# More buffers for scaled weight words and raw heads, and PSUM as the first stop of twenty weight pieces

## Chip, cores and metric

The kernel runs on one core of a Trainium2 chip. The metric is the device time of one execution in microseconds. Before the change it is 1238.18 us (median of 3 runs, 1236.21 to 1244.08).

## The reference

Decayed causal attention over 64 heads (8 batches of 8 heads, 576 tokens of 64 numbers each) is followed by a normalised feed-forward layer on the 4608 tokens of width 512.

```python
# q, k, v: (8, 8, 576, 64); f: (8, 8, 576)
scores = matmul(q, k.T) / 8
cum = cumsum(log(clip(f, 1e-4, 1)))
scores = where(causal, -1e9, scores + cum[:, None] - cum[None, :])
attn = exp(scores - max(scores)); attn = attn / (sum(attn) + 1e-9)
x = matmul(attn, v)                      # heads side by side: (8, 576, 512)
xn = (x - mean(x)) / sqrt(var(x) + 1e-6) * g_ln
out = x + maximum(xn @ w_ch1, 0) @ w_ch2 # w_ch1: 512 x 2048, w_ch2: 2048 x 512
```

The two weight matrices arrive as float64 words. [...]

## The kernel before

**Three streams in one order.** The order of all instructions is written out by hand. Time is cut into slots, four for each head (u counts them, t = 1 to 4 is the slot in the head). In a slot a string of letters (`ORDERS`) says in which order the pieces of work are issued: `W` and the fill letters `w`, `g`, `f` for the weights' preparation, `Q` scores, `S` mask and row minimum, `e` exponential, `B` row sums and scaling, `t`, `h`, `l` transposes of the probabilities and their copies, `A`, `F`, `a` probabilities times v, `P` loads and splits for the next heads, and `M`, `r`, `m`, `N`, `R` the feed-forward part. Each engine runs its own instructions strictly in this order. So does SyncE, which issues every transfer: an issue that has to wait for a buffer holds up all transfers behind it.

**Weights.** The class `WPrep` prepares 32 pieces of 128 x 512, by turns one of the first matrix (layer 1) and one of the second (layer 2). A call of `tick` moves several pieces by one step each. In the order of a piece's life the steps are:

- `load`: SyncE brings 128 x 512 words of 8 bytes into a `wr` buffer (3 of them, lines 147 and 152).
- `scaled` (line 163): ScalarE scales the upper halves and writes them to a `wy` buffer (5 of them, `W_FLOAT`).
- `decode` (lines 173 and 174): VectorE shifts the lower halves in place, then shifts the scaled words and ors the lower halves into them, in place in `wy`. After this the `wr` buffer is free.
- `colsum` and `centre` (lines 186 and 194), for layer 1 alone: TensorE makes column sums, VectorE multiplies by the gains and adds the centring.
- `high` (line 211): ScalarE rounds to the short format that TensorE takes.
- `low` (line 215): GpSimd subtracts the rounded part, which leaves the rest. After this the `wy` buffer is free.
- `keep` (line 220): the rest of layer 2 goes to DRAM.

A layer 2 piece is scaled at the end of one tick, decoded in the next, and its `low` comes three ticks after the decoding; a layer 1 piece takes five. The line that scales piece n + 1 stands in the fill queue of tick n, behind the decoding of piece n.

**Attention.** The first eight heads are plain: their q and k go to the multiplier as they are. From head 8 on q and k are split into a high and a low part. For these heads line 315 allots the `raw` buffer (one), line 316 loads it in slot 4 two heads ahead, `prep_a` to `prep_c` (lines 334 to 346, slots 1 to 3 one head ahead) split it: ScalarE casts into `hi` (lines 334 and 341), GpSimd subtracts (lines 337 and 345). The last of these is also the last use of the `raw` buffer. Scores (lines 365, 367, 368) land in PSUM, VectorE adds the mask (391), ScalarE takes the exponential (402), VectorE adds to the row sum and inverts it (407, 408), GpSimd scales (409), TensorE transposes (415), ScalarE copies out of PSUM (465). Lines 478 and 500 multiply by v; line 531 (`xs`) copies the result out of PSUM.

**Feed-forward.** From slot 35 on (`FIRST_MOE`) chunks of 256 tokens run between the heads: `mm1` (577 to 579), the two parts of the rectified result (585, 590), `mm2` (599 to 601) into two accumulators. These are the two PSUM banks tagged `acc0` and `acc1`, first allotted in `mm2`; the other six banks are shared by everything else under the tag `b`.

Of the kernel before, what the change touches and what calls it, by code (L numbers as in the profile page):

```python
# [8 lines left out]
F32 = mybir.dt.float32  # L9
F32R = mybir.dt.float32r  # L10
U32 = mybir.dt.uint32
I32 = mybir.dt.int32
AF = mybir.ActivationFunctionType
ALU = mybir.AluOpType

B, H, S, D = 8, 8, 576, 64
DM, DFF = H * D, 4 * H * D
P = 128
# [15 lines left out]
WARM = 36  # L34

W_SLOTS, W_CHANGE, W_TICKS = 1.6, 34, 0.95
W_RAW, W_FLOAT = 3, 5
W_BORROW = 2
W_SUMS = 2
W_ASIDE = 5  # L40
FILL = {"f": 3, "g": 2, "w": 1}
RSTD = 6

# [13 lines left out]
def attn_moe(ctx: ExitStack, tc: tile.TileContext, qk, v, f, g, w1, w2, out):  # L59
    nc = tc.nc  # L60
# [4 lines left out]
    ps = ctx.enter_context(tc.tile_pool(name="ps", bufs=1, space=bass.MemoryType.PSUM))  # L65

    wpool = ctx.enter_context(tc.tile_pool(name="early", bufs=1))
    late = ctx.enter_context(tc.tile_pool(name="late", bufs=1))
# [6 lines left out]
    def m2(name, dt):  # L75
        return work.tile([P, 512], dt, tag="m2", bufs=11, name=name)
# [9 lines left out]
    for i in range(WARM):  # L86
# [4 lines left out]
        out=mask[:, S - P :], in_=mask[:, S - P :], pattern=[[-1, P]], base=0,  # L91
# [42 lines left out]
    class WPrep:  # L134
# [8 lines left out]
        def load(self, n):  # L143
            layer, j = self.items[n]
            raw = wpool.tile([P, 2 * DM], U32, tag="wr", bufs=W_RAW, name=f"wr{layer}_{j}")
            if layer == 1:
                nc.sync.dma_start(
                    out=raw.rearrange("p (k f) -> p k f", k=KT),
                    in_=w1.bitcast(U32)[:, 2 * j * P : 2 * (j + 1) * P].rearrange("(k p) f -> p k f", p=P),
                )  # L150
            else:
                nc.sync.dma_start(out=raw, in_=w2.bitcast(U32)[j * P : (j + 1) * P, :])
            halves = raw.rearrange("p (n t) -> p n t", t=2)
            self.d[n] = {"hw": halves[:, :, 1], "lw": halves[:, :, 0]}

        def scaled(self, n):
            layer, j = self.items[n]
            d = self.d[n]
            if layer == 1 and self.tick_no < W_BORROW:
                d["y"] = m2(f"wy{layer}_{j}", U32)  # L160
            else:
                d["y"] = wpool.tile([P, DM], U32, tag="wy", bufs=W_FLOAT, name=f"wy{layer}_{j}")
            nc.scalar.activation(d["y"].bitcast(F32), d["hw"].bitcast(F32), AF.Prelu, scale=2.0**-112, alpha=2.0**32)

        def decode(self, n):
            layer, j = self.items[n]
            d = self.d[n]
            y, low = d["y"], d["lw"]
            d["w"] = y.bitcast(F32)
            ve = nc.vector  # L170

            return [
                lambda: ve.tensor_scalar(out=low, in0=low, scalar1=29, scalar2=None, op0=ALU.logical_shift_right),
                lambda: ve.scalar_tensor_tensor(
                    out=y, in0=y, scalar=3, in1=low, op0=ALU.logical_shift_left, op1=ALU.bitwise_or
                ),
            ]

# [85 lines left out]
        late = None  # L264
# [32 lines left out]
    def new_xq(name, dt):  # L297
        xq = work.tile([66, S], dt, tag="xq", bufs=2, name=name)
        nc.gpsimd.memset(xq[64:66, :].bitcast(F32), 1.0)
        return xq  # L300

    def load(n):
        h = Head()
        h.n, h.plain, h.full = n, n < NPLAIN, n < NFULL
        if h.plain:
            h.kl = work.tile([66, S], F32, tag="kl", bufs=2, name=f"kl{n}")
            if len(xfs) < 2:
                xfs.append(new_xq(f"xf{n}", F32))
            h.xq = xfs[n % 2]
            nc.sync.dma_start(out=h.xq[0:64, :], in_=qk[n][0:64, 0, :])  # L310
            nc.sync.dma_start(out=h.kl[0:64, :], in_=qk[n][0:64, 1, :])
            if n > 0:
                nc.sync.dma_start(out=h.kl[64:66, :], in_=cumd[n])
            return h
        h.raw = late.tile([P, 2, S], F32, tag="raw", bufs=1, name=f"raw{n}")
        nc.sync.dma_start(out=h.raw, in_=qk[n])
        return h

# [316 lines left out]
    def run_later(k):  # L635
        while later and k > 0:
            later.pop(0)()
            k -= 1
# [23 lines left out]
    class Moe:  # L662
# [21 lines left out]
        low = []  # L684
# [63 lines left out]
    def start_head(n):  # L748
        hd[n] = load(n)
# [9 lines left out]
    for u, slot in enumerate(slots):  # L759
# [4 lines left out]
        if slot is not None:  # L764
            n, t = slot
            h = hd[n]
# [6 lines left out]
        def piece(c):  # L773
# [34 lines left out]
            elif c == "L":  # L808
                run_later(RSTD)
            elif c == "M" and want:  # L810
# [38 lines left out]
    while moe.left() > 0 or moe.prev is not None:  # L849
        if moe.can(2 * FT):  # L850
            moe.first()
            moe.first_high()
            moe.first_low()
        run_later(RSTD)
        moe.fetch_low(ALL)
# [40 lines left out]
```

## Time and profile before

| | |
|---|---|
| Median of 3 runs | 1238.18 us |
| Profiled execution | 1240.83 us |
| Its span, first to last instruction | 1239.0 us |
| TensorE busy | 1215.1 us |
| VectorE busy | 767.6 us |
| ScalarE busy | 647.6 us |
| GpSimd busy | 427.3 us |
| Mean granted TensorE clock | 0.988 |

All times in the lines of the profile are microseconds, and `mean ns` is nanoseconds. PE is TensorE's multiplication, PEld its weight loads, DVE is VectorE, ACT ScalarE, POOL GpSimd, SP SyncE; a q behind the name means the sequencer of that engine. `out<-in` names the tiles, and L163 is line 163. A row of a timeline has the start, the duration, the engine and line, and in brackets the idle time of that engine just before it with what ended it. A row of waits has total, number and longest. A row by windows has the window, its length, the busy time of PE, PEld, DVE, ACT and POOL with the number of their instructions, the granted clock, the share of the transfer engines' time, and GB/s. A granted clock of 0.50 means that multiplications ran at half speed.

### The profile page before, as it was taken

The numbers are of one execution on the slowest core, as the hardware profiler recorded it, in microseconds if no ns is written. First come the engines' busy times: TensorE is split into PE (matmuls) and PEld (weight loads), VectorE is DVE, ScalarE is ACT, GpSimd is POOL, SyncE is SP. The second block draws the span as 40 slices with busy tenths as digits, with TensorE's granted clock in tenths as the row PEclk, the third lists the DMA queues.
The fourth block names the chain that finished last, engine by engine and source line by source line (L and its number), as shares of the span: only waits on it lengthen the run. The fifth ranks groups of instructions, "written<-read, shape, count | busy, mean of one in ns | idle before, by whom it ended". The sixth has DMA issues, their size and how long they took to land.

```text
span 1239.0 us, 25554 instructions
## 1 busy us (share of the span) xinstructions
PE 1215.1 (98%) x8140; PEld 1080.7 (87%) x8140; DVE 767.6 (62%) x2884; ACT 647.6 (52%) x1920; POOL 427.3 (34%) x533
## 2 busy tenths in 40 slices
PE   8998999999999999999999999999999999999998
PEld 5555789888999999999999999999999999999997
DVE  5786737576766767676767676767676765233232
ACT  5777655455656555555565555555555653112111
POOL 3567553344333434343433343343444330000000
PEclk8997999999999999999999999999999999999999
DMA  6875744444544554544454554545454543443532
GB/s 181 235 234 179 240 141 133 148 126 140 163 154 154 172 166 148 152 158 142 152 161 155 166 158 145 157 138 160 150 152 145 169 149 103 135 129 111 154 111 94
DMA packets 138359, 190.79 MB, mean 154 GB/s; under 512 B 31216, under 2 KB 80624, under 8 KB 138224
## 3 DMA queue, kind: packets, MB, share of 16 engines
q1 hardware_dynamic: 138224, 189.15, 49.5%
q8 instruction: 65, 1.06, 0.4%
q14 instruction: 70, 0.57, 0.2%
HBM read 157.46 MB, written 23.36 MB: 146 GB/s over the span
## 4 chain that ended last, share of the span: by engine, by line
PE 89%; DVE 3%; ACT 2%; DMA 2%; POOL 1%; issue 1%; SPq 0%; DVEq 0%; POOLq 0%; ACTq 0%
PE h L577 11%; PE h L578 11%; PE h L579 11%; PE acc L599 11%; PE acc L600 10%; PE acc L601 10%; PE tr L415 7%; PE o L500 6%; PE s L367 3%; PE s L368 3%; PE o L478 2%; PE xp L415 1%; DMA raw<-in_qk_dram 1%; PE s L365 1%; PE pc L186 1%
## 5 line engine op out<-in xcount | busy, mean ns | idle before, releaser
L409 POOL TENSOR_SCALAR p<-p,st 64x64 f32<-64x64 f32 (+4 forms) x320 | 171.8, 540 | 555.1 <-DVE st L408 217.9
L577 PE MATMUL h<-x,w1h 128*128 128x256 f32 x1152 | 330.1, 287 | 3.5 <-DVE st L407 2.7
L578 PE MATMUL h<-x,w1h 128*128 128x256 f32 x1152 | 326.2, 283 | 0.9 <-DVE st L407 0.6
L579 PE MATMUL h<-x,w1l 128*128 128x256 f32 x1152 | 325.2, 282 | 0.0
L585 ACT ACTIVATE hh<-h 128x256 fp32r<-128x256 f32 x288 | 110.5, 384 | 281.7 <-PE h L579 280.4
L590 DVE SCALAR_TENSOR_TENSOR hh<-h,hh 128x256 fp32r<-128x256 f32 x288 | 121.5, 422 | 187.0 <-ACT hh L585 174.2
L599 PE MATMUL acc<-w2h,hh 128*128 128x512 f32 x576 | 228.1, 396 | 0.4 <-ACT hh L585 0.4
L600 PE MATMUL acc<-w2s,hh 128*128 128x512 f32 x576 | 226.6, 393 | 0.0
L601 PE MATMUL acc<-w2h,hh 128*128 128x512 f32 x576 | 226.0, 392 | 0.0
L577 PEld LDWEIGHTS h<-x,w1h 128*128 128x128 f32 x1152 | 218.4, 190 | 8.5 <-DVE st L407 3.0
L578 PEld LDWEIGHTS h<-x,w1h 128*128 128x128 f32 x1152 | 218.5, 190 | 4.7 <-DVE x L562 1.7
L579 PEld LDWEIGHTS h<-x,w1l 128*128 128x128 f32 x1152 | 218.3, 189 | 0.0
L402 ACT ACTIVATE p<-p,st 64x64 f32<-64x64 f32 (+4 forms) x320 | 178.3, 558 | 54.0 <-DVE st L391 51.3
L465 ACT CAST ph<-tr 64x128 fp32r<-64x128 f32 (+4 forms) x416 | 117.9, 332 | 131.1 <-PE tr L415 100.8
L415 PE MATMUL tr<-identr,p 128*128 128x128 f32 (+1 forms) x896 | 141.2, 274 | 5.5 <-ACT xs L531 2.3
L391 DVE CUSTOM_DVE_ANT_0 p<-s,mask 64x64 f32<-64x64 f32 (+4 forms) x320 | 130.2, 419 | 7.7 <-PE s L368 2.8
L470 DVE TENSOR_TENSOR ph<-tr,ph 64x192 fp32r<-64x192 f32 x208 | 62.6, 301 | 114.5 <-ACT ph L465 111.6
L601 PEld LDWEIGHTS acc<-w2h,hh 128*128 128x128 f32 x576 | 108.3, 188 | 25.5 <-DVE st L407 0.2
L415 PEld LDWEIGHTS tr<-identr,p 128*128 128x128 f32 (+1 forms) x896 | 101.2, 131 | 29.2 <-POOL p L409 10.3
L599 PEld LDWEIGHTS acc<-w2h,hh 128*128 128x128 f32 x576 | 109.0, 189 | 13.1 <-ACT hh L585 0.6
L600 PEld LDWEIGHTS acc<-w2s,hh 128*128 128x128 f32 x576 | 109.3, 190 | 12.4
L367 PE MATMUL s<-hi 128*64 128x64 f32 x336 | 110.6, 351 | 2.8 <-POOL hi L345 2.6
(80 smaller groups left out, 1805.6 us busy)
## 6 DMA issues: line engine op xcount, KB each, us to landing
w2s<-w2d SPq DMA_DIRECT2D x288, 256.0 KB
raw<-in_qk_dram SPq DMA_DIRECT2D x56, 576.0 KB
wr<-in_w_dram SPq DMA_DIRECT2D x32, 512.0 KB
vr<-in_v_dram SPq DMA_DIRECT2D x64, 160.0 KB
out_dram<-xt SPq DMA_DIRECT2D x36, 256.0 KB
xq<-hi SPq DMA_DIRECT2D x56, 144.0 KB
xa<-xs SPq DMA_DIRECT2D x32, 160.0 KB
w2d<-wl SPq DMA_DIRECT2D x16, 256.0 KB
```

Source lines behind the costliest of these rows:

```text
L367: mm(sp, h.hi[:, 0, q0 : q0 + m], h.hi[:, 1, a:z], start=True, stop=False)
L391: nc.vector.tensor_tensor_reduce(out=pt[:m, a:z], in0=sp, in1=mask[:m, off + a : off + z], scale=-SCALE, scalar=3.0e38 if i == 0 else st[: ...
L402: nc.scalar.activation(pt[:m, :w], pt[:m, :w], AF.Exp, bias=st[:m, i : i + 1], scale=-1.0, accum_out=st[:m, 2:3])
L409: nc.gpsimd.tensor_scalar(out=pt[:m, :w], in0=pt[:m, :w], scalar1=st[:m, 3:4], scalar2=1.0, op0=ALU.mult, op1=ALU.mult)
L415: nc.tensor.transpose(out_, in_, ident[:m, :m])
L577: mm(ph, w1h[:, k, fs], c.x[k][:, 0, :], start=(k == 0), stop=False)
L578: mm(ph, w1h[:, k, fs], c.x[k][:, 1, :], start=False, stop=False)
L579: mm(ph, w1l[:, k, fs], c.x[k][:, 0, :], start=False, stop=(k == KT - 1))
L590: nc.vector.scalar_tensor_tensor(out=h[:, 1, :], in0=ph, scalar=0.0, in1=h[:, 0, :].bitcast(F32), op0=ALU.max, op1=ALU.subtract)
L599: mm(c.acc[i], h[:, 0, ts_], w2h[:, j, :], start=(j == 0), stop=False)
L600: mm(c.acc[i], h[:, 0, ts_], low, start=False, stop=False)
L601: mm(c.acc[i], h[:, 1, ts_], w2h[:, j, :], start=False, stop=(j == FT - 1))
```

## The change

`scaled` writes the first twenty pieces (`W_PSUM`, ten of each layer) to PSUM, to the banks tagged `acc0` and `acc1` by turns. The second instruction of `decode` then reads its first operand there and writes its result to the `wy` buffer, as before. Later pieces are scaled in place as they were. There are nine `wy` buffers and two `raw` buffers. The memory for them comes from the scratch that is set aside for transfers whose descriptors are made on the core: it is set to 1024 bytes. The order of the instructions is the same.

```diff
-W_RAW, W_FLOAT = 3, 5
+W_RAW, W_FLOAT = 3, 9
...
+W_PSUM = 20
...
-            nc.scalar.activation(d["y"].bitcast(F32), d["hw"].bitcast(F32), AF.Prelu, scale=2.0**-112, alpha=2.0**32)
+            d["z"] = d["y"]
+            if n < W_PSUM:
+                d["z"] = ps.tile([P, DM], U32, tag=f"acc{n % 2}", bufs=1, name=f"wz{layer}_{j}")
+            nc.scalar.activation(d["z"].bitcast(F32), d["hw"].bitcast(F32), AF.Prelu, scale=2.0**-112, alpha=2.0**32)
...
-            y, low = d["y"], d["lw"]
+            y, z, low = d["y"], d["z"], d["lw"]
...
-                    out=y, in0=y, scalar=3, in1=low, op0=ALU.logical_shift_left, op1=ALU.bitwise_or
+                    out=y, in0=z, scalar=3, in1=low, op0=ALU.logical_shift_left, op1=ALU.bitwise_or
...
-        h.raw = late.tile([P, 2, S], F32, tag="raw", bufs=1, name=f"raw{n}")
+        h.raw = late.tile([P, 2, S], F32, tag="raw", bufs=2, name=f"raw{n}")
...
-    nc = bacc.Bacc("TRN2", target_bir_lowering=False, num_devices=1)
+    nc = bacc.Bacc("TRN2", target_bir_lowering=False, num_devices=1, dynamic_dma_scratch_size=1024)
```

## The prediction

> **What bounds the kernel now.** I read the page first, then the waits of TensorE and ScalarE in the stage with the idle time, then that stage's timeline engine by engine, last the granted clock in it.
>
> ```profile
> span 1239.0 us, 25554 instructions
> PE 1215.1 (98%) x8140; PEld 1080.7 (87%) x8140; DVE 767.6 (62%) x2884; ACT 647.6 (52%) x1920; POOL 427.3 (34%) x533
> ```
>
> TensorE is busy for 98% of the span, and its instruction order is fixed in the program. So the time is its work, plus its idle time, plus what a lower clock costs. The next rows split the span in three stretches (the busy columns are in the order PE, PEld, DVE, ACT, POOL; then the granted clock).
>
> ```profile
> 7.00:36.00 29.00, 25.07 (x122) 16.62 (x120) 20.02 (x76) 20.12 (x56) 11.27 (x19) 0.88 0.68 197
> 36.00:131.00 95.00, 85.47 (x417) 55.29 (x417) 70.69 (x245) 71.68 (x210) 59.20 (x65) 0.89 0.72 216
> 131.00:1239.00 1108.00, 1099.52 (x7582) 1003.72 (x7580) 674.39 (x2562) 553.27 (x1654) 353.67 (x439) 1.00 0.48 147
> ```
>
> What the change could free for TensorE lies in the middle row: the first holds the start, before the buffers are short, and in the last TensorE idles for under 1%. TensorE idles 95 - 85.5 = 9.5 us and loses 11% of the clock, some 10.4 us. About 20 us is therefore the most that can be won. Without those losses the stage would be 75 us long, with ScalarE busy for 71.7 of them: 95% of a queue that runs in order and waits on others. Winning all of it is unlikely for that reason alone.
>
> **Part 1, nine buffers.** Each weight piece takes a `wy` buffer at line 163 and gives it back when GpSimd has subtracted at line 215. With five, one comes free per tick and one is taken per tick, so the ScalarE instruction waits for the subtraction issued in the same tick. Queued behind it on ScalarE are the copies (`xs`, `ph`) that give PSUM banks back to TensorE. ScalarE's waits in the stage:
>
> ```profile
> ACT wy L163 <- POOL wl L215: 5.1, 5, 2.1
> ACT ph L465 <- PE tr L415: 3.9, 4, 1.5
> ACT wy L163 <- POOL w1l L215: 2.4, 3, 1.0
> ```
>
> Nine buffers cover four more ticks, so all eight waits (7.5 us of ScalarE) go. Only some of them reach TensorE. The first clear one:
>
> ```profile
> 46.35 0.68 ACT L163 ACTIVATE wy<-wr 128x512 f32<-128x512 f32 x1 [1.19 <-POOL wl L215]
> 46.93 0.41 ACT L531 COPY xs<-o 64x320 f32<-64x320 f32 x1
> ```
>
> ```profile
> 47.48 0.49 PE L415 MATMUL tr<-identr,p 128*64 128x128 f32 x3 [1.18 <-ACT xs L531]
> ```
>
> Without the wait, `wy` starts at 45.16 (46.35 - 1.19), `xs` 0.58 later at 45.74 and ends at 46.15, before TensorE gets there at 46.30 (47.48 - 1.18). That gap goes, and with it the half clock that follows:
>
> ```profile
> 48.49:51.91 3.42, 3.42 (x11) 1.68 (x9) 2.36 (x11) 2.29 (x8) 0.53 (x1) 0.50 0.21 80
> 92.87:96.28 3.41, 3.36 (x8) 1.62 (x9) 1.62 (x7) 3.18 (x10) 2.31 (x3) 0.50 0.17 39
> 113.35:123.59 10.24, 9.52 (x35) 7.28 (x36) 6.17 (x19) 7.69 (x23) 8.32 (x8) 0.50 0.67 224
> ```
>
> Half a clock for 3.42 us of matmuls is 1.7 us. 1.18 + 1.71 less 0.1 for the next `ph` copy: **2.8 us**. The second place:
>
> ```profile
> 90.64 0.67 ACT L163 ACTIVATE wy<-wr 128x512 f32<-128x512 f32 x1 [1.20 <-POOL wl L215]
> ```
>
> ```profile
> 91.76 0.49 PE L415 MATMUL tr<-identr,p 128*64 128x128 f32 x3 [1.16 <-ACT xs L531]
> 92.92 0.68 PE L478 MATMUL o<-ph,vr 64*64 64x256 f32 x1 [0.67 <-ACT ph L465]
> ```
>
> The 1.16 goes. The 0.67 behind it stays, because ScalarE still has copies and casts to do first.
>
> ```profile
> 99.20 0.24 PE L367 MATMUL s<-hi 128*64 128x64 f32 x1
> ```
>
> The half clock from 92.87 may go too, yet I count nothing for it: the matmul of 99.20 reads `hi` of raw head 8, which GpSimd makes last in a chain (exponential, row sum, scaling, subtraction) that does not run on TensorE. What TensorE gains on the way it then waits. So **1.16 us**. The third place:
>
> ```profile
> 100.87 0.68 ACT L163 ACTIVATE wy<-wr 128x512 f32<-128x512 f32 x1 [0.33 <-POOL wl L215]
> ```
>
> ```profile
> 103.87 1.16 PE L186 MATMUL pc<-wy,gneg 128*128 128x128 f32 x8 [0.54 <-ACT xs L531]
> 104.87 0.49 PE L415 MATMUL tr<-identr,p 128*64 128x128 f32 x3
> 106.54 0.68 PE L478 MATMUL o<-ph,vr 64*64 64x256 f32 x1 [1.19 <-ACT ph L465]
> ```
>
> The 0.33 stands on ScalarE ahead of the `xs` copy that TensorE awaits for 0.54: **0.3 us**. The longest of the eight, 2.1 us, falls beside the GpSimd chain of part 2, and I count nothing for it.
>
> **Part 2, two raw heads.** The load of raw head n+2 keeps its place in the program, one slot after the last use of head n+1. A second buffer therefore helps only where SyncE stood waiting for that use. This happened once:
>
> ```profile
> SPq L316 <- POOL hi L345: 1.4, 1, 1.4
> ```
>
> ```profile
> 99.18 0.33 SPq L316 DMA_DIRECT2D raw<-in_qk_dram x1
> ```
>
> ```profile
> 103.40 0.42 ACT L531 COPY xs<-o 64x320 f32<-64x320 f32 x1
> 105.11 0.67 ACT L334 CAST hi<-raw 128x576 fp32r<-128x576 f32 x1 [1.29 <-DMA raw<-in_qk_dram]
> ```
>
> It was the load at 99.18, of head 9. It could issue 1.4 earlier, so ScalarE does not stand still for 1.29. Behind that cast queue `wy` and then `ph`, whose input TensorE finished at 105.36 (104.87 + 0.49). With 1.29 less in front of it `ph` is no longer held up by ScalarE but by that end, and of the 1.19 us gap before 106.54 some 0.3 is left, the length of the copy: **0.9 us**. It does not grow from there:
>
> ```profile
> 108.16 0.53 POOL L409 TENSOR_SCALAR p<-p,st 128x320 f32<-128x320 f32 x1 [3.15 <-ACT hi L341]
> 108.66 1.40 POOL L337 TENSOR_TENSOR kl<-raw,hi 64x576 fp32r<-64x576 f32 x1
> 110.02 1.72 POOL L215 TENSOR_TENSOR wl<-wy,w2h 128x512 fp32r<-128x512 f32 x1
> 111.73 0.80 POOL L409 TENSOR_SCALAR p<-p,st 128x448 f32<-128x448 f32 x1
> 112.61 1.40 POOL L345 TENSOR_TENSOR hi<-raw,hi 64x576 fp32r<-64x576 f32 x1
> ```
>
> ```profile
> 114.07 0.31 PE L367 MATMUL s<-hi 128*64 128x64 f32 x1 [2.56 <-POOL hi L345]
> ```
>
> GpSimd runs without a break from 108.16 to 114.0, and TensorE waits for its end. Its start moves by the same 0.9. Whatever else TensorE wins before (the half clock at 106.5 too) turns into a longer wait here, from 2.56 towards 4 us. The smaller scratch costs nothing: all data goes by the hardware queue, and no transfer is issued by GpSimd.
>
> **Part 3, twenty pieces in PSUM.** No row of before has ScalarE write scaled words to PSUM, or this shift-and-or read them there. The nearest rows:
>
> ```profile
> L174 DVE SCALAR_TENSOR_TENSOR wy<-wy,wr x32: 676/912/2074, 8.4 to 155.0; 128x512 uint32<-128x512 uint32 x32
> 0.00:98.60 98.60, 20.66 (x20) 0.93 0.70 208
> L658 DVE SCALAR_TENSOR_TENSOR xt<-acc,rs,xt x36: 740/744/751, 204.7 to 1235.3; 128x512 f32<-128x512 f32 x36
> L163 ACT ACTIVATE wy<-wr x32: 643/666/710, 7.4 to 152.5; 128x512 f32<-128x512 f32 x32
> L173 DVE TENSOR_SCALAR wr<-wr x32: 407/412/1476, 7.8 to 154.0; 128x512 uint32<-128x512 uint32 x32
> ```
>
> Line 174 reads two SBUF tensors and spreads from 676 to 2074 ns; line 658 has the same shape and reads one of the two from PSUM, and keeps to 740 to 751. The first twenty (the second row, of line 174 alone) took 20.66 us. At 0.744 they take 14.9: **5.8 us of VectorE**; the bounds are 20 x 0.676 (7.1 saved) and no change. ScalarE's own instruction I leave at 0.666; 20 times its spread is from 0.5 us gained to 0.9 lost. VectorE has 24 us free in the stage, so most of this lies beside other work. It can only count where TensorE waits on a chain through VectorE:
>
> ```profile
> 80.60 0.27 PE L415 MATMUL tr<-identr,p 128*64 128x128 f32 x1 [0.67 <-DVE st L391]
> ```
>
> I give it **0.2 us** of this gap; 0 and 0.67 are its ends.
>
> The Trainium skill (SBUF — State Buffer, section Who interferes with whom) says that a VectorE instruction with two SBUF inputs contends with a GpSimd instruction that reads SBUF, and that a `tensor_scalar` in its two-port mode does so too. By the first sentence the spread of line 174 ends for all twenty, as the rows suggest. By the second, which speaks against the change, line 173 in front of it (407 to 1476 ns in its row) stays exposed. The page has no price for that; the sum above does not use it.
>
> Two waits are added. Line 163 of piece n waits until line 174 of piece n-2 has read the bank, and the first `mm2` of the feed-forward part waits for pieces 18 and 19. Behind the first stand `xs`, `ph` and the exponentials, behind the second all of TensorE. Both are long over:
>
> ```profile
> L174 DVE SCALAR_TENSOR_TENSOR wy<-wy,wr x3: 679/815/1464, 83.2 to 91.5; 128x512 uint32<-128x512 uint32 x3
> L599 PE MATMUL acc<-w2h,hh x1: 396/396/396, 132.1 to 132.1; 128*128 128x512 f32 x1
> ```
>
> Pieces 17 to 19 are read at 83.2 to 91.5. Piece 17 is through at 84.7, 4.8 us before line 163 of piece 19 could run (89.4), and the first accumulation starts 40 us later.
>
> **Sum:** 2.8 + 1.16 + 0.3 + 0.9 + 0.2 = 5.4 us. The profiled execution took 1240.8 us and its span was 1239.0, so it becomes 1235.4. It was 2.6 us above the median of the runs, 1238.2; from the median the forecast is **1232.8 us**.
>
> **Rivals.** *All of it is won.* If ScalarE and GpSimd keep up, the stage loses its 9.5 us of idle time and the 10.3 us of half clock: 1238.2 - 19.8 = 1218.4. For it: eight ScalarE waits and 5.8 us of VectorE go at once. Against it: the unbroken GpSimd chain above and the 95%. A part way, 9 to 14 us, is likelier than the end.
>
> *Another wait takes over.* TensorE arrives earlier and waits for the exponentials or for `hi`; the half clocks return at new gaps. Gain 0 to 3 us, 1235 to 1238. For it: in the stage ScalarE is already busy for 75% and the chain passes from engine to engine.
>
> *Slower, by the clock.* The gap in front of 114.07 grows from 2.6 towards 4 us. The half clock after it, three windows of 3.41 us, could last longer while TensorE's matmuls there are on the path. Each window more costs 1.7 us, so from four more (6.8 us against 5.4) the kernel is slower: 1238.2 + 1.4 = 1239.6, two more still 1243. For it: the 10.24 us row, against single windows elsewhere. Against it: TensorE is nearly always busy after 114, and then single windows were enough. The Trainium skill (TensorE: Matmul & The Clock Gate, section What's actually happening) has full clock return after one busy window of about 3.4 us; by that rule this case has no room. The trace agrees at 48.49 and 92.87 and disagrees at 113.35, where three windows passed with 9.5 of 10.2 us busy.
>
> *The second raw buffer does nothing* (the load waits for bandwidth): 0.9 less, 1233.7, inside the forecast's own range.
>
> **How the numbers follow.** One per cent, 12.4 us, is about what a measurement of this kernel can tell from no change. Forecast (3 to 9 us gained) 0.50; most of it won (9 to 20) 0.25, of which over 12.4 us 0.17; another wait (0 to 3) 0.17; slower 0.08, of which over 1% 0.04. So faster 0.17, same 0.79, slower 0.04. The range runs from 1225, 13 us gained, to 1241, where the clock case begins to cost; the unknown prices of part 3 move it by under 2 us.
>
> **What would show it.** Right: no wait of line 163 on line 215 in the waits; line 174's first twenty near 0.745 us with no spread; no gap and full clock at the first place; raw head 9 issued within 0.5 us of the weight load ahead of it; and a wait for `hi` of about 4 us still there before the matmul of 114.07, now about 5 us earlier. Wrong: that wait gone or the middle stage shorter by over 9 us (GpSimd did not bind), a new ScalarE wait on the weight loads, or the 131 to 1239 stage changed by over 2 us, for which I have no cause.

## The result and the profile after

The median is 1233.24 us (1229.54 to 1236.59, 11 runs) against 1240.27 us for the kernel before over 11 runs beside it (1236.21 to 1244.08). The ratio is 0.9944 (95% interval 0.9935 to 0.9954), which is 6.9 us faster (5.7 to 8.1), where 5.4 us were forecast. (The 1232.8 us of the forecast were counted from the median of three runs of before, which lies 2.1 us below that of the eleven.) The profiled execution of after has a span of 1233.4 us, 5.6 us less than that of before.

The page of after, and its three stretches (window, length, busy time of PE, PEld, DVE, ACT, POOL, granted clock, transfer share, GB/s):

```profile
span 1233.4 us, 25519 instructions
PE 1209.6 (98%) x8140; PEld 1079.6 (88%) x8140; DVE 763.8 (62%) x2884; ACT 647.0 (52%) x1920; POOL 425.6 (35%) x533
```

```profile
7.00:36.00 29.00, 24.36 (x113) 16.64 (x111) 18.00 (x71) 17.87 (x50) 10.37 (x17) 0.82 0.62 176
36.00:131.00 95.00, 86.69 (x468) 58.45 (x467) 71.81 (x271) 76.23 (x226) 61.46 (x70) 0.96 0.80 240
131.00:1233.40 1102.40, 1093.51 (x7542) 999.48 (x7540) 671.39 (x2542) 550.43 (x1645) 350.62 (x436) 1.00 0.47 147
```

In the middle stretch TensorE now does 468 multiplications in 95 us where it did 417, but these are not the same ones. Between the same two matmuls, the last of them the first of the feed-forward part, before and after read:

```profile
25.95:130.57 104.62, 95.09 (x466) 61.14 (x464) 78.13 (x273) 79.64 (x233) 64.08 (x71) 0.90 0.70 211
28.03:124.29 96.26, 87.95 (x467) 58.16 (x465) 72.15 (x272) 78.56 (x232) 62.58 (x71) 0.96 0.77 229
```

Of the 8.4 us between them most is clock: two windows of 3.41 us at half clock instead of six, which is worth 6.8 us. The idle time is hardly less, 8.3 against 9.5 us.

**The buffer wait is gone.** ScalarE's waits from 28 to 131 us (total, number, longest) have no line any more in which the scaling (now L167) waits for GpSimd's subtraction (now L219):

```profile
ACT p L406 <- DVE st L395: 8.0, 12, 1.5
ACT w1h L215 <- DVE wy L198: 3.7, 5, 1.0
ACT ph L469 <- PE tr L419: 3.7, 6, 0.8
ACT hi L338 <- DMA raw<-in_qk_dram: 2.3, 2, 1.9
ACT xs L535 <- PE o L482: 1.5, 2, 0.8
ACT wy L167 <- DMA wr<-in_w_dram: 1.1, 1, 1.1
```

At the first place the scaling follows the exponential at once, `xs` follows it, and TensorE's transposes start without a gap (ScalarE, then TensorE):

```profile
46.35 0.19 ACT L406 ACTIVATION_READ_ACCUMULATOR p<-p,st 128x1 f32 x1
46.44 0.63 ACT L167 ACTIVATE wz<-wr 128x512 f32<-128x512 f32 x1
47.01 0.41 ACT L535 COPY xs<-o 64x320 f32<-64x320 f32 x1
```

```profile
48.04 0.57 PE L419 MATMUL tr<-identr,p 128*64 128x128 f32 x3
```

**The operations that PSUM changed.** By line, with minimum, median and maximum in ns; `wz` are the twenty pieces that go through PSUM, `wy<-wy,wr` the twelve that don't:

```profile
L178 DVE SCALAR_TENSOR_TENSOR wy<-wz,wr x20: 674/684/692, 8.4 to 89.0; 128x512 uint32<-128x512 uint32 x20
L178 DVE SCALAR_TENSOR_TENSOR wy<-wy,wr x12: 676/1284/2070, 95.3 to 149.1; 128x512 uint32<-128x512 uint32 x12
```

```profile
L167 ACT ACTIVATE wz<-wr x20: 602/626/649, 7.0 to 87.3; 128x512 f32<-128x512 f32 x20
L167 ACT ACTIVATE wy<-wr x12: 650/664/677, 91.6 to 146.1; 128x512 f32<-128x512 f32 x12
```

The spread of the shift-and-or ends, as the Trainium skill's rule on two SBUF inputs has it (SBUF — State Buffer, section Who interferes with whom). It is even faster than the 745 ns that I took from the other operation with a PSUM input. The shift in place ahead of it (now L177, 409/417/1620 ns) still spreads, as it did before (407/412/1476).

**The wait for GpSimd has grown.** Two score matmuls wait for `hi` of the first split heads, and GpSimd's chain before the second has no gap, as before:

```profile
96.35 0.24 PE L371 MATMUL s<-hi 128*64 128x64 f32 x1 [1.60 <-POOL hi L349]
...
108.77 0.24 PE L371 MATMUL s<-hi 128*64 128x64 f32 x1 [3.64 <-POOL hi L349]
```

```profile
102.86 0.54 POOL L413 TENSOR_SCALAR p<-p,st 128x320 f32<-128x320 f32 x1 [0.84 <-ACT hi L345]
103.36 1.41 POOL L341 TENSOR_TENSOR kl<-raw,hi 64x576 fp32r<-64x576 f32 x1
104.73 1.71 POOL L219 TENSOR_TENSOR wl<-wy,w2h 128x512 fp32r<-128x512 f32 x1
106.42 0.81 POOL L413 TENSOR_SCALAR p<-p,st 128x448 f32<-128x448 f32 x1
107.32 1.40 POOL L349 TENSOR_TENSOR hi<-raw,hi 64x576 fp32r<-64x576 f32 x1
```

**The raw load.** Head 9's load is issued 0.45 us after the weight load ahead of it (SyncE), and ScalarE casts it without standing still:

```profile
92.91 0.40 SPq L148 DMA_DIRECT2D wr<-in_w_dram x1
93.36 0.49 SPq L320 DMA_DIRECT2D raw<-in_qk_dram x1
```

```profile
99.78 0.67 ACT L338 CAST hi<-raw 128x576 fp32r<-128x576 f32 x1
```

**A loss that I did not foresee.** Later, in the feed-forward part, TensorE stops for 4.1 us. Its line of before had 2.73 us at the same matmul. In front of it ScalarE stands still for the load of raw head 17 (3.84 us before):

```profile
241.65 0.67 ACT L338 CAST hi<-raw 128x576 fp32r<-128x576 f32 x1 [5.20 <-DMA raw<-in_qk_dram]
```

```profile
244.47 0.58 PE L581 MATMUL h<-x,w1h 128*128 128x256 f32 x1 [4.08 <-DVE st L411]
```

**The clock.** The three stretches of half clock at 48.5, 92.9 and 106.5 are gone, the one behind 110 is two windows long instead of three. Two others are one window longer: at the start (two windows before) and behind the stop near 244 (one before).

```profile
17.77:28.01 10.24, 9.63 (x30) 6.56 (x31) 6.86 (x26) 6.02 (x19) 3.43 (x6) 0.50 0.50 151
28.01:109.93 81.92, 75.15 (x406) 49.03 (x405) 62.49 (x243) 68.11 (x202) 52.17 (x62) 1.00 0.78 232
109.93:116.76 6.83, 6.83 (x25) 4.59 (x24) 3.85 (x13) 5.24 (x16) 6.42 (x7) 0.50 0.53 196
243.05:249.88 6.83, 5.42 (x19) 4.84 (x20) 4.28 (x16) 3.62 (x11) 3.16 (x5) 0.50 0.36 121
```

Since TensorE's order is the same, the start of the same matmul in both traces shows where the 5.6 us between these two executions came from:

| up to the matmul at (before / after) | change in this stretch | forecast |
|---|---|---|
| 25.9 / 28.0 | +2.1 | 0 |
| 51.9 / 50.8 (past the first place) | -3.2 | -2.8 |
| 91.8 / 88.9 (past the second place) | -1.8 | -1.16 - 0.2 |
| 99.2 / 96.4 (`hi` of head 8) | 0.0 | 0 |
| 106.5 / 101.8 (past raw head 9) | -1.9 | -0.3 - 0.9 |
| 114.1 / 108.8 (`hi` of head 9) | -0.5 | 0 |
| 130.6 / 124.3 (feed-forward begins) | -1.0 | 0 |
| 249.3 / 244.5 (the later stop) | +1.4 | 0 |
| end | -0.7 | 0 |

### The profile page after: what moved, and what is told of

It is laid out like the page before. It is cut to its first block, busy times and chain, and to the rows that moved or that the text cites. A ratio compares the mean times of both kernels' runs of the same rounds, so it can differ in the third digit from the quotient of the medians.

```text
span 1233.4 us, 25519 instructions
## 1 busy us (share of the span) xinstructions
PE 1209.6 (98%) x8140; PEld 1079.6 (88%) x8140; DVE 763.8 (62%) x2884; ACT 647.0 (52%) x1920; POOL 425.6 (35%) x533
## 4 chain that ended last, share of the span: by engine, by line
PE 91%; DVE 3%; DMA 2%; ACT 2%; SPq 1%; issue 1%; POOL 0%; DVEq 0%; ACTq 0%; POOLq 0%
PE h L581 11%; PE h L582 11%; PE h L583 11%; PE acc L603 11%; PE acc L604 10%; PE acc L605 10%; PE tr L419 7%; PE o L504 6%; PE s L371 3%; PE s L372 3%; PE o L482 3%; PE s L369 2%; DMA raw<-in_qk_dram 1%; PE xp L419 1%; PE pc L190 1%; DMA wr<-in_w_dram 1%
```

## The experiments

All ratios are to the kernel before on the same chip, with 95% intervals; 0.001 is 1.24 us.

| kernel | ratio | interval |
|---|---|---|
| whole change | 0.9944 | 0.9935 to 0.9954 |
| e1 nine buffers alone | 0.9970 | 0.9954 to 0.9985 |
| e2 two raw buffers alone | 1.0002 | 0.9990 to 1.0015 |
| e3 PSUM alone | 0.9970 | 0.9957 to 0.9982 |
| e6 whole change, six buffers | 0.9936 | 0.9919 to 0.9954 |
| e8 six buffers, first stop in SBUF | 0.9960 | 0.9945 to 0.9974 |
| e10 whole change, one raw buffer | 0.9955 | 0.9938 to 0.9972 |
| e5 subtractions of heads 8, 9 on VectorE | 0.9957 | 0.9941 to 0.9974 |
| e4 raw loads two slots earlier | 0.9893 | 0.9875 to 0.9910 |
| e7 e4 and e5 together | 0.9904 | 0.9886 to 0.9921 |
| e9 two raw buffers and early loads alone | 0.9948 | 0.9931 to 0.9964 |

My theory was the sum of the prediction: the buffer wait carries the gain, PSUM next to nothing. The rival was that VectorE's freed time carries it.

**e1, nine buffers alone**

```diff
-W_RAW, W_FLOAT = 3, 5
+W_RAW, W_FLOAT = 3, 9
```

(and the smaller scratch of the change, as in e2 and e9)

> Nine wy buffers alone; one raw buffer, nothing in PSUM. My theory (the ScalarE waits for GpSimd's subtraction reach TensorE at three places: 2.8 + 1.2 + 0.3 us): 4.3 us faster than before, ratio 0.9965; no wait of the scaling on the subtraction is left, the gap before the transposes near 47.5 and the half clock after it are gone. The rival that VectorE's freed 5.8 us carries the gain: under 2 us faster here.

Measured 3.7 us (1.9 to 5.7): the size is that of the theory. But the gaps at the first and at the second place are only halved, and what ends them is another engine; the gap that was 0.67 us at 80.60 is longer. TensorE in e1:

```profile
47.95 0.69 PE L415 MATMUL tr<-identr,p 128*64 128x128 f32 x2 [0.61 <-POOL p L409]
...
79.96 0.49 PE L415 MATMUL tr<-identr,p 128*64 128x128 f32 x3 [0.92 <-DVE st L391]
90.51 0.81 PE L415 MATMUL tr<-identr,p 128*64 128x128 f32 x3 [0.61 <-POOL p L409]
```

ScalarE is no longer late there; GpSimd's scaling of the probabilities is. So the wait was handed on, and nine buffers do not close these gaps by themselves. At the third place they do more than I counted: the gaps of 0.54 and 1.19 us before 103.87 and 106.54 are both gone with one raw buffer, and ScalarE stands still for raw head 9 for 0.16 us instead of 1.29.

**e2, two raw buffers alone**

```diff
-        h.raw = late.tile([P, 2, S], F32, tag="raw", bufs=1, name=f"raw{n}")
+        h.raw = late.tile([P, 2, S], F32, tag="raw", bufs=2, name=f"raw{n}")
```

> Two raw buffers alone. My theory: the load of raw head 9 is issued 1.4 us earlier and the result is 0.9 us faster at most, not to be told from no change (0.9990 to 1.0000). The rival that a second raw buffer feeds all 56 heads earlier (35 of them waited, 39 us of ScalarE in all): 3 us or more faster, and the total wait for raw loads shorter.

No change (1.0002). The 1.19 us gap at the matmul of 106.54 is gone here too, yet the next wait takes it. The rival is out too: ScalarE's waits for raw loads are no shorter (42.7 us, 39.1 before). TensorE in e2, first the old place, then the score matmul of head 9:

```profile
49.52 0.49 PE L415 MATMUL tr<-identr,p 128*64 128x128 f32 x3 [1.18 <-ACT xs L531]
...
113.62 0.32 PE L367 MATMUL s<-hi 128*64 128x64 f32 x1 [4.16 <-POOL hi L345]
```

The first of these lines tells something else. It is the gap of before, 1.18 us, and in before half a clock followed it. Here none did:

```profile
45.20:48.61 3.41, 3.13 (x15) 1.61 (x13) 3.10 (x14) 2.22 (x10) 2.65 (x3) 1.00 1.07 238
48.61:52.02 3.41, 2.40 (x11) 1.34 (x12) 3.22 (x10) 3.41 (x11) 2.15 (x4) 1.00 0.82 266
52.02:55.43 3.41, 3.41 (x23) 2.74 (x22) 2.40 (x12) 2.12 (x8) 1.46 (x3) 1.00 0.47 123
```

The windows of 3.41 us have edges of their own: counted on from the half clocks of e2's trace, which begin at 17.89 and 113.47 us (28 windows apart), an edge falls at 48.61 and cuts the gap in two. In e9, which has five `wy` buffers as well and the same gap of 1.18 us before 48.80, two windows of half clock followed, of which this is the first:

```profile
50.71:54.13 3.42, 3.42 (x10) 2.08 (x9) 2.25 (x10) 2.17 (x7) 1.17 (x3) 0.50 0.14 36
```

So the half clock behind this gap was one window in before, none in e2 and two in e9: the 1.71 us that I counted differ from execution to execution.

**e3, PSUM alone.** The diff of the change without its first and its `raw` line.

> Twenty pieces scaled into PSUM, five wy buffers, one raw buffer. The wait for a wy buffer moves from the scaling on ScalarE to the shift-and-or on VectorE for these twenty pieces, since that is now the first to write the buffer. My theory, which did not think of this: 0.2 us. The new rival: as ScalarE no longer waits, most of the nine buffers' gain comes here too, 3 us or more, and VectorE shows the waits instead. Line of the shift-and-or for the twenty near 0.745 us each in both.

Measured 3.7 us (2.2 to 5.3): the rival of this run is right, my 0.2 us was wrong. ScalarE waits for a `wy` buffer only at four of the pieces after the twentieth, 4.2 us in all (9.4 us in e2's trace, which has the old five buffers), since the buffer is now first written by VectorE later on. VectorE shows no wait for it either. How much of the 3.7 us comes from this and how much from the faster shift-and-or is not shown. The first gap is closed whole:

```profile
47.71 0.56 PE L419 MATMUL tr<-identr,p 128*64 128x128 f32 x3
```

**e6, six buffers instead of nine**

```diff
-W_RAW, W_FLOAT = 3, 9
+W_RAW, W_FLOAT = 3, 6
```

> All of the change but with six wy buffers instead of nine. If the wait was for a subtraction of the same tick only, one buffer more is one tick more (some 4.5 us) and six do as well as nine: the same ratio as the whole change, 0.994. If the subtraction is later than a tick, part of the gain is lost.

As the whole change (0.9936). Beside the stop in PSUM one buffer more is enough, and the other three bring nothing. Six buffers without that stop, under which VectorE takes the buffer a tick later, were not run.

**e8, the same stop in SBUF.** This tells apart the two things that PSUM does.

```diff
-                d["z"] = ps.tile([P, DM], U32, tag=f"acc{n % 2}", bufs=1, name=f"wz{layer}_{j}")
+                d["z"] = wpool.tile([P, DM], U32, tag=f"wz{n % 2}", bufs=1, name=f"wz{layer}_{j}")
```

(with six `wy` buffers, to be held against e6)

> The whole change with six wy buffers, but the first stop of the twenty pieces is two buffers of their own in SBUF instead of the two PSUM banks: the same waits and buffers as with PSUM, yet the shift-and-or reads two SBUF tensors again. New theory (what PSUM brings is the end of the contention between VectorE's two-input reads and GpSimd): the shift-and-or spreads to 2 us again and the ratio falls back to that of nine buffers alone, 0.997. Rival (it is the separate first stop, which frees ScalarE from the buffer): 0.994, as with PSUM.

The shift-and-or of the same twenty pieces spreads again, and the gaps of e1 are back (0.62, 0.98 and 0.58 us). The first is ended by the same instruction of GpSimd. By line, then TensorE, in e8:

```profile
L178 DVE SCALAR_TENSOR_TENSOR wy<-wz,wr x20: 676/820/1956, 7.9 to 91.8; 128x512 uint32<-128x512 uint32 x20
```

```profile
48.65 0.80 PE L419 MATMUL tr<-identr,p 128*64 128x128 f32 x3 [0.62 <-POOL p L413]
```

GpSimd is late there for two reasons. VectorE's shift-and-or some 6 us earlier takes longer, and behind it on VectorE stand the mask and the row sums that the exponentials and then GpSimd's scaling wait for; and GpSimd's own subtraction right ahead takes longer. VectorE and GpSimd in e8, then in e6:

```profile
40.63 1.47 DVE L178 SCALAR_TENSOR_TENSOR wy<-wz,wr 128x512 uint32<-128x512 uint32 x1
46.42 1.71 POOL L219 TENSOR_TENSOR wl<-wy,w2h 128x512 fp32r<-128x512 f32 x1
```

```profile
40.55 0.68 DVE L178 SCALAR_TENSOR_TENSOR wy<-wz,wr 128x512 uint32<-128x512 uint32 x1
45.62 1.28 POOL L219 TENSOR_TENSOR wl<-wy,w2h 128x512 fp32r<-128x512 f32 x1
```

The contention theory holds at these places: same buffers, same waits, other memory, and both engines are late again. In the total the ratio (0.9960) lies on its side, but the intervals of e6 and e8 overlap (0.9945 to 0.9954), so the 3 us between them are likely and not shown.

**e10, the whole change with one raw buffer**

```diff
-        h.raw = late.tile([P, 2, S], F32, tag="raw", bufs=2, name=f"raw{n}")
+        h.raw = late.tile([P, 2, S], F32, tag="raw", bufs=1, name=f"raw{n}")
```

> The whole change with one raw buffer. If the second buffer is worth nothing at the place where the load stands, the ratio is that of the whole change, 0.994; if it earns its 0.9 us only once ScalarE and VectorE are free, 0.995 and the wait for raw head 9 is back on ScalarE.

0.9955, with an interval that holds both 0.9944 and 1 us more. The wait for raw head 9 is not back on ScalarE: its cast at 99.44 us follows the copy ahead of it without a wait. With e1 and e2: where the load stands in the program, the second buffer earns nothing that can be measured.

**e5, two subtractions moved off GpSimd**

```diff
-        nc.gpsimd.tensor_tensor(
+        (nc.vector if h.n in (8, 9) else nc.gpsimd).tensor_tensor(
             out=h.kl[0:64, :], in0=h.raw[0:64, 1, :], in1=h.hi[0:64, 1, :].bitcast(F32), op=ALU.subtract
```

(and the same for `hi`)

> The whole change, and the two subtractions that split heads 8 and 9 run on VectorE instead of GpSimd (0.75 us each by the rows of the same kind, not 1.4). My theory (GpSimd's unbroken chain sets when the first score matmul of head 9 starts): the waits for these parts, 1.6 and 3.6 us, shrink to under 1.5 us together and the half clock behind them goes: 3 to 6 us faster than the whole change, ratio 0.990 to 0.992. Rival (ScalarE, busy without a break there, is next in line): under 2 us.

Half of it came true. TensorE's waits from 90 to 131 us in e5:

```profile
PE pc L190 <- ACT xs L535: 1.3, 2, 1.0
PE s L371 <- DVE hi L349: 1.2, 2, 0.8
PE tr L419 <- DVE wy L198: 0.9, 1, 0.9
```

The wait for `hi` fell from 5.2 to 1.2 us. The time did not (0.9957, not better than the whole change): ScalarE's copies and VectorE's own work are late next, as the rival had it, and the half clock did not go: three windows of it between 100 and 121 us, where the whole change had two. GpSimd did end that wait, but with ScalarE busy for 74 of 95 us (36 to 131) it is not the only bound of this stage.

**e4, the raw loads in slot 2**

```diff
-                if t == 4 and NPLAIN <= n + 2 < B * H:
+                if t == 2 and NPLAIN <= n + 2 < B * H:
                     start_head(n + 2)
```

> The whole change, and the loads of raw heads are issued in slot 2 instead of slot 4, which only the second buffer allows. If the stop of 4.1 us before the feed-forward matmul near 244 comes from the raw load landing after ScalarE wants it, ScalarE's wait for raw loads (35 to 40 us in all) goes and with it that gap and its half clock: 4 to 6 us faster than the whole change, ratio 0.990 to 0.991. The rival that the transfers are late for want of bandwidth: no change from 0.994.

0.9893: 6.3 us better than the whole change, 13.3 us better than before, and the lowest ratio of the study. ScalarE's wait for raw loads (39.1 us before, 45.2 us after) has no line in it any more, the stop near 244 is gone, and TensorE idles for 4.2 us after 131 instead of 8.9:

```profile
131.00:1223.20 1092.20, 1088.03 (x7530) 995.61 (x7528) 667.83 (x2536) 549.08 (x1637) 349.86 (x436) 1.00 0.48 148
```

**e7, e4 and e5 together**

> Both of these together. If they act at different places, near 107 and near 244, the gains add: 7 to 11 us faster than the whole change, ratio 0.985 to 0.989. If one wait only hands over to the next, it is no better than the better of the two.

No better than e4 alone (0.9904): e5 has nothing to add.

**e9, the second raw buffer with early loads, without the other two parts**

> The kernel before with two raw buffers and the loads of raw heads in slot 2; five wy buffers, nothing in PSUM. If the early load works at its own place (the stop near 247 and its half clock), it brings the 6 us here too that it brought on top of the whole change: ratio 0.9945 to 0.996. If it needs the other two parts, under 3 us.

0.9948: 6.4 us. With the 6.9 us of the whole change this makes the 13.3 us of e4, so the two act at different places and add. The traces say the same: between the matmuls at 200 and 300 us of before, TensorE is 6.6 us faster in e9 and in e4. The early load has a small price: TensorE now waits once for the transfer of `xq` (0.7 us in e4, 1.9 us in e9).

## Why the prediction was right, and where it was not

*What bounds.* TensorE's fixed order, its idle time and its clock in the stage up to 131 us: right. The gain lies there (-8.4 us from 26 to 131), and two other stretches gave 3.5 of it back. Its make-up was another: the terms hold some 3.7 us of idle time and 1.7 of clock, the traces 1.2 and 6.8. What TensorE won in idle time before, it mostly lost to longer waits for `hi` (5.2 us against 2.6), as the prediction itself had said. The clock's part is not the change's alone: e2's trace is 3.9 us shorter in this stretch, with a single half window behind 110 us, and its runs show no gain.

*Nine buffers, 4.3 us.* Right in size (3.7 us alone), with the eight waits gone as told, but in part by luck, since each of its terms was off. At the first and the second place the buffers alone close half of each gap; the other halves need PSUM (e1, e8). At the third, 1.7 us of gaps went where 0.3 was counted (e1). And the 1.71 us of half clock changes with the execution (none in e2, two windows in e9), so it should have stood in the sum as a chance, not as a whole.

*Two raw heads, 0.9 us.* The step was right at its own place and wrong in the sum. The load came earlier and ScalarE's stop was gone, but alone it measured nothing (1.0002). I had written myself that GpSimd's chain follows and takes what TensorE wins, and still added the 0.9. Beside nine buffers there was nothing left to win: they close the same gap with one raw buffer (e1), and e10 leaves it closed.

*PSUM, 0.2 us.* This is the step that failed: "It can only count where TensorE waits on a chain through VectorE". It measured 3.7 us alone and some 3 us beside nine buffers (likely and no more, since the intervals of e1 and of e8 touch or overlap those of the kernels with PSUM). I priced VectorE's freed time and looked for TensorE waiting on VectorE itself, where I found one gap and gave it 0.2 us. That gap is closed whole (0.92 us in e1, none in after). And VectorE is late further up the chain: its slower shift-and-or delays what GpSimd's scaling waits for, and while VectorE's two-input read runs, GpSimd's subtraction takes longer too, so that TensorE waits for GpSimd at two more places. The three gaps make 2.1 us in e1 and 2.2 in e8, and none is left in after; the rest of the 3 us was not traced. I also missed that the first writer of a `wy` buffer changes from ScalarE to VectorE, which takes the buffer wait off ScalarE without any further buffer (e3).

*No gain from the half clock at 92.9, a wait for `hi` of about 4 us.* Right: 1.60 and 3.64 us, and the stretch up to 99.2 changed by nothing.

*The stage after 131 us.* I had said that a change of over 2 us there would have no cause that I know. Before and after differ by +1.4 us up to the matmul near 249 (+0.7 to the end). The cause is the raw load again: it is issued one slot ahead of its use, so TensorE, arriving earlier, waits longer for ScalarE, which waits for the load. e4 shows it by taking it away. The +2.1 us at the start are in part a third window at half clock. They differ from execution to execution: e2, whose edit touches nothing there but the size of the scratch, has +1.9 us and three windows, e5, which holds the whole change, +0.5 and two.

The total came out near because errors cancelled: PSUM was worth some 3 us more than forecast, the raw buffer 0.9 and the nine buffers 0.6 less, and in the traces compared the later stop and the start gave back 3.5.

*The rivals.* "Another wait takes over" was true at several places, for a part of the gain. The slower case by the clock did not come: behind 110 there were two half windows instead of three.

## What to carry to other kernels

Contention between VectorE and GpSimd costs on both sides: price it by what waits for GpSimd too, and by what waits further down the chain. A PSUM stop for one operand ends it for that instruction, not for its neighbours that work in SBUF. A second buffer is worth what the program then does with it: here nothing where the load stood, and 6 us when the load was moved into the room that it made. A gap on the bounding engine that several engines share is closed only when the last of them is early, so take the next releaser into the sum before a gain is added.

## What the runs showed of the hardware

- ScalarE writes 128 x 512 words to PSUM in 626 ns, to SBUF in 664 ns.
- VectorE's shift-and-or with one operand in PSUM takes 684 ns, about as long as the fastest with both in SBUF (676 ns), while the multiply-add of line 658 with one PSUM operand takes 744 ns.
- Half the clock can follow a window of 3.41 us in which TensorE was idle for 1.3 us (before, up to 48.49; e9, up to 50.71), and need not: in after the window from 92.87 to 96.28 held 1.5 us of idle time, and the clock stayed whole. What else the window held seems to count; this was not settled. The Trainium skill's account (TensorE: Matmul & The Clock Gate, section What's actually happening), a whole idle window of about 3.4 us before the clock drops, does not fit the first of these.
